# A planned attention-and-MLP kernel: P as a ring of 18 blocks, another rule for VectorE's score steps, another price for an exponential

## The chip, the cores and the metric

One core of one Trainium2 chip. The time is the device time of one execution in microseconds (us), as a median of runs. Engines: TensorE (PE; its weight loads are listed as PEld), VectorE (DVE), ScalarE (ACT), GpSimd (POOL), and SyncE (SP), which issues most DMAs. PSUM has eight banks of 512 fp32 columns, numbered 0 to 7 below.

## What is computed

Cut to what matters (S = 2048, D = 512, 32 heads of 16, one shared K and V head; Fh = 688):

```python
q = (x @ wq) -> 32 heads;  k = x @ wk;  v = x @ wv
p = softmax(einsum('bhqd,bkd->bhqk', q, k) * 16 ** -0.5)
a = einsum('bhqk,bkd->bhqd', p, v) -> (S, 512) @ wo
z = gelu(x @ w_in);  z1, z2 = z[..., :Fh], layernorm(z[..., Fh:])
b = (z1 * (w_sp @ z2 + b_sp[:, None])) @ w_out
g = sigmoid((x * gate_w).sum(-1, keepdims=True))
out = g * a + (1 - g) * b
```

All inputs and the output are bf16.

## The kernel before

**Units and blocks.** The attention is cut into 32 units: a unit u is one chunk of 512 queries and four heads. A *block* is one head's scores of a unit against 128 keys: a matmul of K (32 x 128) and Q (32 x 512) gives a bank of 128 keys x 512 queries (`s_mm`, rows `ps<-QA,KA`). Four heads stand in the four row groups of TensorE, so up to four such matmuls, one for each group g, run side by side. A unit has 16 key tiles x 4 heads = 64 blocks, and the whole kernel 2048.

**Two ways to an exponential.** Most blocks go to ScalarE: one instruction of two or three banks writes exp to the buffer P (`exp_op`, L738, rows `P<-ps`). The step number k sets its banks, `EB[k % 2]`: banks 2 and 3 (and 4, if it is free) or banks 0 and 1. The rest of the key tiles, at most 8 per unit, go to VectorE as a polynomial: `d_A` (L750) evacuates a block from bank 5 or 4 (`DBK`) with a scale and an offset into UW, `d_u` (L757) squares it, and `d_w` (L763) squares it again, on VectorE or, one block of 512 columns at a time, on GpSimd. Where a second matmul's weights and constants complete the polynomial, TensorE adds small matmuls (`UW,VW`, `QA,KTV`, `CT,SVB`). A key tile of VectorE is called a batch; `batches` counts them.

**P·V.** `o_mm` multiplies a block of P or UW by V, in bank 6, one column group per head. Four such matmuls, one of each head, make a round (`pv_round`, `pv_emit`). At a unit's end VectorE transposes bank 6 (`T`, L775), normalises it with GpSimd's help and transposes it back into OT (L806).

**The other half.** z = gelu(x @ w_in) is computed on TensorE between score steps; all gelu instructions of ScalarE run in one stretch, since they need another activation table. After the layernorm come `g_sp` (`wT,z`) and the output matmuls (`wout,z` and `wo,OT`). These groups (`main`, `outs`, `tails`) are called fill: TensorE works at them one piece at a time.

**The order is planned.** No engine chooses anything at run time. While the program is built, a loop steps three clocks (`free`, for pe, act and dve) in nanoseconds, asks `pe_step`, `act_step` or `dve_step` what its engine does next, and records that instruction; each has a due time from constants such as `C_MM = 216.0`. The recorder `Prog.op` then derives semaphore waits from who wrote and read each key. So a constant of the planner changes the order of the instructions and their split between the engines, not the instructions' own speed. The engines run their lists in order.

**The parts that the change touches:**
- P is `[128, NP, 1536]` with NP = 6: step k uses slot k % 6, whether it fills two or three blocks. Reads and writes are tracked per slot (`("P", k % NP)`), `pleft[k]` counts the blocks of a step that P·V has not read yet, and `act_step` does not plan step k before step k - 6 is fully read.
- `act_period(n)`: 426.7 n + 58 ns, the planned distance of two exponentials of n blocks.
- `pe_work`: after ScalarE's next score step (`if bl:`, which also takes along blocks for VectorE while `d_ready` holds) comes a branch for score blocks of VectorE alone (`if d_ready(now, False)`). It is taken in score mode ("S"), where TensorE has just run scores and need not switch, or when no step of ScalarE is open, in the gelu stretch, or when VectorE is short of work.
- `hungry(now)` is VectorE's planned backlog in ns; so far it only decides on bank 4.
- P·V rounds with fewer than four heads are allowed if `press` holds: the slots of P are nearly all in use.
- A filler matmul on zeros (`CT,zer`, tag "warm") is put in where TensorE's planned load over the last 3.4 us is below `W_MIN`.
- `unit_for_act`, `new_batch`: which key tiles VectorE takes. A tile of the next unit is only taken while more than 64 - 12 of its blocks are left.

At the end (`put_out`) the rows of the output are stored by SP, ACT and POOL queues. A flag of the polynomial's validity is read by all engines; a second program, with its own P·V (L1690), runs only if it is set.

Of the kernel before, what the change touches and what calls it, by code (L numbers as in the profile page):

```python
# [6 lines left out]
ACT = mybir.ActivationFunctionType  # L7
# [7 lines left out]
S = 2048  # L15
# [5 lines left out]
NST = 16  # L21
NU = 32
LN_EPS = 1e-5
NP = 6
ND = 5
NQ = 3
NMAX = 8
Q_B = 0.74
Q_A = 0.4770697274170593
Q_AS = 0.5048945666981567  # L30
# [12 lines left out]
RLAST = 12  # L43
XO = (0, 3, 2, 1)
N0 = 3
HEAD = 45000.0
C_TN = 1250.0
GATE = 20000.0
# [4 lines left out]
WBL = 0.5  # L53
BACK = 8
W_WIN = 3400.0
W_MIN = 0.84
W_GEL = 0.95
INFO = None

# [106 lines left out]
def build_kernel(nc, x_d, wq_d, wk_d, wv_d, wo_d, win_d, wsp_d, bsp_d, wout_d, gw_d, out_d):  # L166
    es = ExitStack()
    with es:
        block = es.enter_context(nc.Block())

        def sb(name, shape, dt):
            return es.enter_context(nc.sbuf_tensor(name, shape, dt))
# [9 lines left out]
        def bkey(b):  # L182
            return ("bk", b)
# [14 lines left out]
        NE = sb("NE", [128, 4, 32], B16)  # L198
        SVB = sb("SVB", [128, NMAX + 1, 32], B16)
        CT = sb("CT", [128, 512], B16)  # L200
        P = sb("P", [128, NP, 1536], B16)
        UW = sb("UW", [128, 2, ND, 2048], F16)
        T1 = sb("T1", [128, 2, 512], F32)
        rc = sb("rc", [128, 2, 16], F32)
# [528 lines left out]
            mm(bank(dst_bank), KA[32 * g:32 * g + 32, e, 128 * kt:128 * kt + 128], QA[32 * g:32 * g + 32, (u // 2) % NQ, :], True, True,  # L733
               kr + [("Q", (u // 2) % NQ)], [key], tp=(32 * g, 0), chan="s", tag="S")

        def exp_op(k, n):
            b0, _ = EB[k % 2]
            op("act", lambda a: a.activation(P[:, k % NP, 0:512 * n], ps[:, 512 * b0:512 * (b0 + n)], ACT.Exp),  # L738
               r=[bkey(b0 + i_) for i_ in range(n)], w=[("P", k % NP)], tag="exp")

        started = set()

# [161 lines left out]
        sdone = {}  # L904
        estart = {}
        eend = {-1: 0.0, -2: 0.0}
        pleft = {}
        db = {"cur": None, "todo": []}
        dbs = {b: {"free": 0.0, "blk": None, "ready": None, "k": None} for b in DBK}
        batches = []  # L910
# [19 lines left out]
        def new_batch(now):  # L930
            if db["todo"]:
                return True
            m = len(batches)
            if m >= ND and dleft.get(m - ND, 0) > 0:
                return False
            ua = unit_for_act()
            for u in (ua, ua + 1):
                if u >= NU:
                    continue
                un = units[u]  # L940
                if un["n"] >= NMAX:
                    continue
                rem = rem_of(u)
                if u == ua and rem < (RLAST if u == NU - 1 else RMIN) + 4:
                    continue
                if u > ua and rem <= 64 - 12:
                    continue
                q = when(("Q", u // 2), ("K%d" % (u % 2), 3))
                if q is None or q > now:
                    continue  # L950
                if max(un["nx"]) >= un["hi"]:
                    continue
                kt = NKT - 1 - un["n"]
                if u == 0:
                    ix = O0.index(kt)
                    if kt < NKT - N0 or max(un["nx"]) > ix:
                        continue
                    O0.pop(ix)
                un["hi"] -= 1
                un["n"] += 1  # L960
                batches.append((u, kt, []))
                dleft[m] = 8
                pq[m] = [0, 0, 0, 0.0, 0.0, 0]
                db["cur"] = m
                db["todo"] = [0, 1, 2, 3]
                return True
            return False
# [18 lines left out]
        def hungry(now):  # L986
            return max(0.0, free["dve"] - now) + dve_backlog(now) + 600.0 * sum(d["blk"] is not None for d in dbs.values())
# [54 lines left out]
            return bl  # L1042

        def act_period(n):
            return 426.7 * n + 58.0

        def limit(now):
            k = st_["kf"]
# [42 lines left out]
        def pv_emit(pu, rnd, t_end):  # L1091
            for g, it in rnd:
                pv_items[pu][g].remove(it)
                pv_done[pu] += 1
                pv_g[pu][g] += 1
                it[1](st_["ua"] > pu and pv_g[pu][g] == unit_total(pu) // 4)
                if it[3] is not None:
                    kind, ix = it[3]
                    if kind == "P":
                        pleft[ix] -= 1  # L1100
                        if pleft[ix] == 0:
                            T[("Pfree", ix)] = t_end + 250.0
                    else:
                        dleft[ix] -= 1
            tot = unit_total(pu)
            if pv_done[pu] == tot and pv_const[pu]:
                st_["pu"] += 1
                unit_end(pu, t_end + L_PE)
# [166 lines left out]
        def pe_work(now):  # L1275
# [9 lines left out]
            def sw(m):  # L1285
                return 0.0 if m == mode else C_SW
# [46 lines left out]
                    return t_end  # L1333
            if d_ready(now, False):
                slack = max(0.0, free["dve"] - now) + dve_backlog(now)
                if mode == "S" or topen is None or gst["on"] or (slack < D_SL and now + sw("S") + C_MM <= lim + C_SW):
                    t_end = now + sw("S") + C_MM
                    used = []
                    while d_ready(now, False):
                        used.append(d_emit(used, now, t_end))  # L1340
                    st_["mode"] = "S"
                    return t_end
# [13 lines left out]
            if pv is not None:  # L1356
                rnd, tot, mx = pv
                pu = st_["pu"]
                oldest = min([ix for ix in pleft if pleft[ix] > 0] or [10 ** 9])
                press = st_["ke"] + 1 - oldest >= NP  # L1360
                ending = st_["ua"] > pu and unit_total(pu) - pv_done[pu] <= tot + 8
                urgent = press or ending
            defer = fp is not None and fp[2] is None and not urgent and pv is not None and tot < BACK
# [23 lines left out]
        def act_step(now):  # L1387
            if not st_["gate"]:
                t = when("KTV", "SVB", *[("V", c) for c in range(4)])
                if t is not None and t < now + GATE:  # L1390
                    st_["gate"] = True
                    gate()
                    return now + 130.0
            if aevac_q and aevac_q[0][2] <= now:
                c_, f_, t, d_ = aevac_q.popleft()
                f_()
                if d_:
                    d_(now + c_ + 100.0)
                return now + c_
            if gst["arm"] and (gel or dz["i"] < 24 or dz["cur"] is not None or dz["full"]) and st_["ke"] == st_["kf"] or gst["on"]:  # L1400
                r = None
                extra = 0.0 if gst["on"] else 1300.0
                if dz["full"] and dz["full"][0][3] <= now + extra:
                    r = dz_act(now + extra)
                elif gel:
                    c_, f_, _ = gel.popleft()
                    f_()
                    r = now + c_ + extra
                if r is None:
                    return None  # L1410
                gst["on"] = True
                gst["t"] = r
                if not (gel or dz["i"] < 24 or dz["cur"] is not None or dz["full"]):
                    gst["on"] = False
                    r += 1300.0
                return r
            k = st_["ke"]
            if k in sdone and sdone[k] <= now:
                bl = stepb[k]
                if k >= NP and (pleft.get(k - NP, 0) > 0 or T.get(("Pfree", k - NP), 0.0) > now):  # L1420
                    return None
                n = len(bl)
                exp_op(k, n)
                pleft[k] = n
                st_["ke"] += 1
                estart[k] = now
                eend[k] = now + 426.7 * n + 172.0
                for i_, (u, kt, g) in enumerate(bl):
                    src = P[:, k % NP, 512 * i_:512 * i_ + 512]
                    add_item(u, g, (eend[k] + L_X,  # L1430
                                    lambda last, u=u, g=g, kt=kt, src=src, k=k: o_mm(u, g, V1[:, kt, :], src, [("V", kt // 4), ("P", k % NP)], last), ("V", kt // 4), ("P", k)))
                if st_["ua"] >= NU and st_["kf"] == k + 1:
                    T[("Bend", k % 2)] = eend[k] + L_X
                    T[("Bend", 1 - k % 2)] = eend[k - 1] + L_X
                return now + act_period(n)
            return None
# [218 lines left out]
        for u in range(NU):  # L1655
# [30 lines left out]
            for kt in range(NKT):  # L1686
                for g in range(4):
                    mm2(bank(g), KA[32 * g:32 * g + 32, 0, 128 * kt:128 * kt + 128], QA[32 * g:32 * g + 32, 0, :], True, True, ["Q"], ["sc"], (32 * g, 0))
                for h in range(2):
                    op2("act", lambda a, h=h: a.activation(P[:, h, 0:1024], ps[:, 1024 * h:1024 * h + 1024], ACT.Exp), r=["sc"], w=["P"])  # L1690
                for g in range(4):
                    mm2(ps[32 * g:32 * g + 32, 512 * BO:512 * BO + 512], V1[:, kt, :], P[:, g // 2, 512 * (g % 2):512 * (g % 2) + 512],
                        kt == 0, kt == 15, ["P"], [("bk", BO)], (0, 32 * g))
            t1_op(ps2, u)()
            jj, jp = j % 2, j // 2
# [105 lines left out]
```

## Time and profile before

| | us |
|---|---|
| median of 3 runs | 746.19 (745.87 to 746.45) |
| the profiled execution | 748.75 |
| its span, first to last instruction | 746.7 |

| engine | busy us | share of the span |
|---|---|---|
| PE | 727.3 | 97% |
| DVE | 710.2 | 95% |
| ACT | 727.3 | 97% |
| POOL | 232.9 | 31% |

How to read the rows that follow. A group row names line, engine, operation, written and read tiles and shape, then the count, busy time in us and mean ns of one instruction, then the idle time of the engine ahead of them and who ended it. A timeline row begins with its start and length in us and merges like neighbours; it has the shape of its first instruction. A row of windows has the stretch, its length, the busy time (and count) of PE, PEld, DVE, ACT and POOL, the granted TensorE clock, the DMA share and GB/s. Since neighbours on an engine overlap, mean ns times count is more than busy time. Matmul ends are modelled, so a busy PE is not a full PE.

### The profile page before, as it was taken

What the parts mean: (1) busy time and instruction counts of PE and PEld (TensorE: products, weight loads), DVE (VectorE), ACT (ScalarE), POOL (GpSimd) and SP (SyncE); (2) the same over time, 40 slices, a digit from 0 to 9 for tenths busy, and PEclk for the clock granted to TensorE, in tenths of its full rate; (3) what the DMA queues carried; (4) which work ended last, traced back from release to release, by engine and by line L of the source; (5) the groups of instructions that cost most, each with busy time, mean ns of one, the idle gap of its engine ahead of it and who ended that gap; (6) DMA issues with size and microseconds to landing.
All of it is one profiled execution on the core that took longest, in us unless ns stands there. A gap on an engine that the chain in (4) does not pass through costs nothing.

```text
span 746.7 us, 21174 instructions
## 1 busy us (share of the span) xinstructions
PE 727.3 (97%) x8969; PEld 212.0 (28%) x8969; DVE 710.2 (95%) x980; ACT 727.3 (97%) x749; POOL 232.9 (31%) x241
## 2 busy tenths in 40 slices
PE   8999999999999999999999999999999999999996
PEld 2323233323323222222222222222222222222221
DVE  5799999998999999999999999999999999999996
ACT  5999999999999999999999999999999999999995
POOL 4744324360222322436223343212215131150101
PEclk8999999999999999999999999999999999999999
DMA  8350000000000000500000051000001400000001
GB/s 185 105 113 2 2 3 1 2 2 2 2 2 1 2 2 2 115 21 9 2 1 2 3 92 44 9 3 1 2 2 29 100 8 9 2 3 1 2 2 33
DMA packets 48445, 17.20 MB, mean 23 GB/s; under 512 B 44164, under 2 KB 47800, under 8 KB 48344
## 3 DMA queue, kind: packets, MB, share of 16 engines
q1 hardware_dynamic: 46040, 15.36, 9.0%
q8 instruction: 71, 1.16, 0.7%
q10 hardware_dynamic: 2256, 0.30, 0.3%
q14 instruction: 30, 0.25, 0.1%
q0 software_dynamic: 48, 0.13, 0.0%
HBM read 3.20 MB, written 2.10 MB: 7 GB/s over the span
## 4 chain that ended last, share of the span: by engine, by line
PE 60%; ACT 21%; DVE 11%; issue 8%; POOL 0%; ACTq 0%; POOLq 0%; DVEq 0%
PE ps L348 59%; ACT P L738 20%; DVE UW L750 4%; DVE UW L757 2%; DVE UW L763 1%; DVE bst L592 1%; PE ps L347 1%; DVE T L775 1%; DVE z L578 0%; DVE QA L465 0%; ACT z L586 0%; POOL UW L763 0%; DVE km L447 0%; ACT z L1265 0%; DVE mv L596 0%
## 5 line engine op out<-in xcount | busy, mean ns | idle before, releaser
L738 ACT ACTIVATE P<-ps 128x1024 bf16<-128x1024 f32 (+1 forms) x729 | 701.1, 1242 | 8.0 <-PE ps L348 7.8
L750 DVE TENSOR_SCALAR UW<-ps 128x512 f16<-128x512 f32 (+1 forms) x409 | 329.7, 818 | 14.9 <-PE ps L348 9.9
L348 PE MATMUL ps<-QA,KA 32*128 32x512 bf16 x2048 | 313.0, 386 | 9.5 <-ACT P L738 6.0
L763 POOL TENSOR_TENSOR UW<-UW 128x512 f16<-128x512 f16 x86 | 130.1, 1512 | 308.0 <-DVE UW L750 131.6
L348 PE MATMUL ps<-P,V 128*32 128x512 bf16 x1532 | 224.4, 387 | 0.4 <-DVE T L775 0.2
L348 PEld LDWEIGHTS ps<-QA,KA 32*128 32x128 bf16 x2048 | 84.2, 91 | 307.9 <-ACT P L738 163.1
L757 DVE TENSOR_TENSOR UW<-UW 128x2048 f16<-128x2048 f16 (+1 forms) x147 | 159.9, 1088 | 1.5
L763 DVE TENSOR_TENSOR UW<-UW 128x2048 f16<-128x2048 f16 (+3 forms) x143 | 136.6, 963 | 0.9 <-POOL UW L763 0.8
L348 PE MATMUL ps<-wT,z 128*32 128x512 bf16 x1536 | 131.9, 383 | 0.0
L348 PE MATMUL ps<-UW,VW 128*32 128x512 f16 x516 | 99.9, 385 | 0.0
L348 PE MATMUL ps<-UW,V 128*32 128x512 f16 x516 | 85.3, 387 | 0.5 <-DVE UW L757 0.4
L348 PEld LDWEIGHTS ps<-P,V 128*32 128x32 bf16 x1532 | 54.3, 94 | 60.5 <-issue 53.2
L469 POOL TENSOR_TENSOR QSQ<-QA 128x512 bf16<-128x512 bf16 x16 | 26.1, 1629 | 84.1 <-DVE UW L750 43.4
L348 PEld LDWEIGHTS ps<-wT,z 128*32 128x32 bf16 x1536 | 32.5, 95 | 38.6 <-issue 34.2
L348 PE MATMUL ps<-wout,z 128*32 128x512 bf16 x384 | 33.3, 383 | 0.0
L798 POOL TENSOR_TENSOR Tn<-T,rc 128x512 bf16<-128x512 f32 x15 | 28.2, 1879 | 9.7 <-DVE UW L750 8.9
L348 PEld LDWEIGHTS ps<-UW,VW 128*32 128x32 bf16 x516 | 24.7, 94 | 20.5 <-issue 15.6
L348 PE MATMUL ps<-win,xT 128*32 128x344 bf16 x512 | 30.2, 313 | 0.0
L348 PEld LDWEIGHTS ps<-UW,V 128*32 128x32 bf16 x516 | 20.7, 93 | 24.1 <-issue 17.5
L811 POOL TENSOR_SCALAR gtmp<-T,thr 128x32 f32<-128x32 f32 x16 | 6.7, 418 | 66.3 <-DVE T L775 65.5
L348 PE MATMUL ps<-QA,KTV 128*32 128x512 bf16 x128 | 25.9, 383 | 0.0
L348 PE MATMUL ps<-xT,win 128*32 128x512 bf16 x384 | 24.0, 381 | 0.7 <-ACT z L1265 0.7
(115 smaller groups left out, 401.9 us busy)
## 6 DMA issues: line engine op xcount, KB each, us to landing
out_dram<-outsb SPq DMA_DIRECT2D x14, 128.0 KB, 1.7
win<-in_B_w_in_dram SPq DMA_DIRECT2D x1, 1376.0 KB, 6.0
wout<-in_B_w_out_dram SPq DMA_DIRECT2D x1, 640.0 KB, 5.2
wo<-in_A_wo_dram SPq DMA_DIRECT2D x8, 64.0 KB, 2.3
UW<-in_A_wq_dram SPq DMA_DIRECT2D x1, 384.0 KB, 4.1
wT<-in_B_w_sp_dram SPq DMA_TRANSPOSE x16, 4.4
UW<-in_A_wq_dram ACTq DMA_DIRECT2D x1, 128.0 KB, 4.0
out_dram<-outsb ACTq DMA_DIRECT2D x1, 128.0 KB, 3.7
```

The source lines that it names most:

```text
L347: return t.matmul(dst, lhsT, rhs, start=start, stop=stop)
L348: return t.matmul(dst, lhsT, rhs, start=start, stop=stop, tile_position=tp)
L469: dq(pl_q, 1050.0, lambda: op("pool", lambda v: v.tensor_tensor(QSQ[:, q % 2, :], QA[:, q % NQ, :], QA[:, q % NQ, :], ALU.mult), r=[("Q", ...
L592: dq(dve_q, 410.0, lambda st=st, h=h: op("dve", lambda v: v.bn_stats(bst[:, st, h, :], z2[:, FH * st + 344 * h:FH * st + 344 * h + 344]), ...
L738: op("act", lambda a: a.activation(P[:, k % NP, 0:512 * n], ps[:, 512 * b0:512 * (b0 + n)], ACT.Exp), r=[bkey(b0 + i_) for i_ in range(n)] ...
L750: op("dve", lambda v: v.tensor_scalar(UW[:, 0, s, 512 * i:512 * (i + n)], bank(b, 512 * n), Q_A, Q_AS, ALU.mult, ALU.add), r=[bkey(b + j) ...
L757: op("dve", lambda v: v.tensor_tensor(src, src, src, ALU.mult), r=k, w=k, tag="dTT")
L763: op(eng, lambda v: v.tensor_tensor(UW[:, 1, s, 512 * a:512 * b], src, src, ALU.mult), r=[("U", s, h) for h in range(a // 2, (b + 1) // 2) ...
L775: return lambda: pgx.op("dve", lambda v: v.transpose(T1[:, jj, c0:c1], bank(BO, c1 - c0, c0)), r=[bkey(BO)], w=[("T1", jj, c0)], tag="T1")
L798: pgx.op(eng, lambda v: v.tensor_tensor(tnv[:, pr, j0:j1, b0:b1, :], t1v[:, j0:j1, b0:b1, 0:16], rc[:, j0:j1, b0:b1].unsqueeze(3).broadcas ...
L811: op("pool", lambda v: v.tensor_scalar(gtmp[:], t1v[:, jj, :, 17:19], thr[:, 0:1], None, ALU.is_le), r=[("T1", jj, 0), "thr"], w=["gtmp"], ...
```

## The change

P becomes one line of 18 blocks of 512 columns. An exponential of n blocks takes the next n of them in a row (from the start again where n do not fit), and each block is released by its own P·V matmul. `press` holds when five or fewer blocks are free. The planned distance of two exponentials is 426.7 n + 52 ns (`A_OV`). In score mode VectorE's blocks alone are taken only if `hungry(now)` is under 1000 ns (`D_HG`). `W_MIN` goes from 0.84 to 0.86; the 12 in `new_batch` gets a name and stays 12.

```diff
-NP = 6
+PB = 18
+PRESS = 5
+NXT = 12
+A_OV = 52.0
+D_HG = 1000.0
-W_MIN = 0.84
+W_MIN = 0.86
...
-        P = sb("P", [128, NP, 1536], B16)
+        P = sb("P", [128, 512 * PB], B16)
...
-        def exp_op(k, n):
+        def exp_op(k, n, p0):
             b0, _ = EB[k % 2]
-            op("act", lambda a: a.activation(P[:, k % NP, 0:512 * n], ps[:, 512 * b0:512 * (b0 + n)], ACT.Exp),
-               r=[bkey(b0 + i_) for i_ in range(n)], w=[("P", k % NP)], tag="exp")
+            op("act", lambda a: a.activation(P[:, 512 * p0:512 * (p0 + n)], ps[:, 512 * b0:512 * (b0 + n)], ACT.Exp),
+               r=[bkey(b0 + i_) for i_ in range(n)], w=[("P", p0 + i_) for i_ in range(n)], tag="exp")
...
-        pleft = {}
+        pbusy_ = [False] * PB
+        pfree_ = [0.0] * PB
+        ppos = [0]
+
+        def p_alloc(n, now):
+            p0 = ppos[0] if ppos[0] + n <= PB else 0
+            if any(pbusy_[i] or pfree_[i] > now for i in range(p0, p0 + n)):
+                return None
+            return p0
...
         def act_period(n):
-            return 426.7 * n + 58.0
+            return 426.7 * n + A_OV
...
                     if kind == "P":
-                        pleft[ix] -= 1
-                        if pleft[ix] == 0:
-                            T[("Pfree", ix)] = t_end + 250.0
+                        pbusy_[ix] = False
+                        pfree_[ix] = t_end + 250.0
...
-                if mode == "S" or topen is None or gst["on"] or (slack < D_SL and now + sw("S") + C_MM <= lim + C_SW):
+                if mode == "S" and hungry(now) < D_HG or topen is None or gst["on"] or (slack < D_SL and now + sw("S") + C_MM <= lim + C_SW):
...
-                oldest = min([ix for ix in pleft if pleft[ix] > 0] or [10 ** 9])
-                press = st_["ke"] + 1 - oldest >= NP
+                press = PB - sum(pbusy_) <= PRESS
...
-                if k >= NP and (pleft.get(k - NP, 0) > 0 or T.get(("Pfree", k - NP), 0.0) > now):
+                n = len(bl)
+                p0 = p_alloc(n, now)
+                if p0 is None:
                     return None
-                n = len(bl)
-                exp_op(k, n)
-                pleft[k] = n
+                exp_op(k, n, p0)
+                ppos[0] = p0 + n
+                for i_ in range(n):
+                    pbusy_[p0 + i_] = True
...
-                    src = P[:, k % NP, 512 * i_:512 * i_ + 512]
+                    src = P[:, 512 * (p0 + i_):512 * (p0 + i_) + 512]
                     add_item(u, g, (eend[k] + L_X,
-                                    lambda last, u=u, g=g, kt=kt, src=src, k=k: o_mm(u, g, V1[:, kt, :], src, [("V", kt // 4), ("P", k % NP)], last), ("V", kt // 4), ("P", k)))
+                                    lambda last, u=u, g=g, kt=kt, src=src, ix=p0 + i_: o_mm(u, g, V1[:, kt, :], src, [("V", kt // 4), ("P", ix)], last), ("V", kt // 4), ("P", p0 + i_)))
```

The second program's use of P is rewritten for the new shape in the same way.

More of the change, by code (lines that the diff above doesn't have):

```diff
@@ L945, in new_batch @@
                     continue
-                if u > ua and rem <= 64 - 12:
+                if u > ua and rem <= 64 - NXT:
                     continue
@@ L1689, in build_kernel @@
                 for h in range(2):
-                    op2("act", lambda a, h=h: a.activation(P[:, h, 0:1024], ps[:, 1024 * h:1024 * h + 1024], ACT.Exp), r=["sc"], w=["P"])
+                    op2("act", lambda a, h=h: a.activation(P[:, 1024 * h:1024 * h + 1024], ps[:, 1024 * h:1024 * h + 1024], ACT.Exp), r=["sc"], w=["P"])
                 for g in range(4):
-                    mm2(ps[32 * g:32 * g + 32, 512 * BO:512 * BO + 512], V1[:, kt, :], P[:, g // 2, 512 * (g % 2):512 * (g % 2) + 512],
+                    mm2(ps[32 * g:32 * g + 32, 512 * BO:512 * BO + 512], V1[:, kt, :], P[:, 512 * g:512 * g + 512],
                         kt == 0, kt == 15, ["P"], [("bk", BO)], (0, 32 * g))
```

## The prediction

> **What bounds the kernel now.** The page's busy shares come first. They do not name a bound: three engines stand within two points of each other.
>
> ```profile
> PE 727.3 (97%) x8969; PEld 212.0 (28%) x8969; DVE 710.2 (95%) x980; ACT 727.3 (97%) x749; POOL 232.9 (31%) x241
> ```
>
> So the second view is ScalarE's timeline, merged: one row for each stretch in which it never stood still, with the idle time ahead of it in brackets.
>
> ```profile
> 9.79 5.28 ACT L738 ACTIVATE P<-ps 128x1536 bf16<-128x1536 f32 x5 [5.51 <-PE ps L348]
> 15.53 1.94 ACT L738 ACTIVATE P<-ps 128x1024 bf16<-128x1024 f32 x2 [0.46 <-PE ps L348]
> 17.77 1.02 ACT L738 ACTIVATE P<-ps 128x1024 bf16<-128x1024 f32 x1 [0.31 <-PE ps L348]
> 19.29 1.02 ACT L738 ACTIVATE P<-ps 128x1024 bf16<-128x1024 f32 x1 [0.49 <-PE ps L348]
> 20.80 10.57 ACT L738 ACTIVATE P<-ps 128x1024 bf16<-128x1024 f32 x10 [0.49 <-PE ps L348]
> ...
> 58.75 2.36 ACT L738 ACTIVATE P<-ps 128x1536 bf16<-128x1536 f32 x2 [0.40 <-PE ps L348]
> 61.28 112.78 ACT L738 ACTIVATE P<-ps 128x1024 bf16<-128x1024 f32 x119 [0.16 <-PE ps L348]
> 174.08 1.28 ACT L586 ACT_TABLE_LOAD   x1
> ...
> 195.01 2.14 ACT L1265 ACTIVATE z<-ps 128x1536 bf16<-128x1536 f32 x2 [0.53 <-PE ps L348]
> ...
> 198.46 539.33 ACT L738 ACTIVATE P<-ps 128x1024 bf16<-128x1024 f32 x562
> ```
>
> From 61.28 us to the gelu at 174.08 us, and from 198.46 to 737.79 us, ScalarE goes from one exponential into the next with no gap. A row can hide stalls inside it if instructions stretch, so the third view is the pace: two stretches with 1024-column exponentials alone, and the groups by shape of the last long stretch.
>
> ```profile
> 105.07 41.56 ACT L738 ACTIVATE P<-ps 128x1024 bf16<-128x1024 f32 x45
> ...
> 541.33 41.62 ACT L738 ACTIVATE P<-ps 128x1024 bf16<-128x1024 f32 x45
> ```
>
> ```profile
> L738 ACT ACTIVATE P<-ps 128x1024 bf16<-128x1024 f32 x504 | 478.5, 1206 | 0.0
> L738 ACT ACTIVATE P<-ps 128x1536 bf16<-128x1536 f32 x57 | 92.5, 1622 | 0.0
> L738 ACT ACTIVATE P<-ps 128x512 bf16<-128x512 f32 x1 | 0.8, 812 | 0.0
> ```
>
> A mean duration of 1206 ns is not the pace, because neighbours overlap. The pace is (41.62 - 1.21) / 44 = 0.918 us per 1024-column instruction, and from the 539.33 us stretch (539.33 - 0.8 - 504 x 0.918) / 57 = 1.331 us per 1536-column one. The difference for 512 more columns is 0.413 us, so a 1024-column instruction is some 0.83 us of columns and under 0.1 us of its own: there is no room for a stall in it. Whose turn is late shows in the waits, as total us, times, longest:
>
> ```profile
> PEld ps L348 <- ACT P L738: 164.4, 386, 1.3
> PEld ps L348 <- DVE UW L750: 82.3, 207, 1.1
> ...
> ACT P L738 <- PE ps L348: 7.8, 7, 5.5
> ```
>
> TensorE's weight loads are released by ScalarE 386 times; ScalarE waits seven times, all of them in the rows above, up to 61.28 us. ScalarE's string of exponentials sets the time; TensorE and VectorE fit around it.
>
> **Removed, added, moved.** The planner runs while the program is built, so the costs come from the built order of both kernels (counts, no times). Exponentials of 1024 columns go from 651 to 670, of 1536 from 76 to 66, of 512 stay 2: 9 more instructions and 8 more blocks of 512 columns, 1532 to 1540. These are two key tiles of four blocks that VectorE's polynomial gives up (129 tiles to 127). On ScalarE this is 19 x 0.918 - 10 x 1.331 = 17.4 - 13.3 = **+4.1 us**, all on the path. The stretch at 105.07 us gives 0.917 and 1.340 us by the same steps, and 17.4 - 13.4 = 4.0; these are the bounds.
>
> [...]
>
> The ring itself: block-wise release can only help an exponential that waits for its place in P. Such a wait would be among the seven waits above, and these are at 9.79 to 61.28 us. TensorE's order is the same in both programs up to the matmuls of this row, where 24 become 20, so the first five waits stand ahead of the first change:
>
> ```profile
> 23.67 0.32 PE L348 MATMUL ps<-V,KN 128*32 128x32 bf16 x24
> ```
>
> The wait that the ring adds is for the last reader of the blocks to be overwritten; behind it on ScalarE queue the next exponentials, and TensorE's scores wait for those. But 18 blocks hold nine exponentials of 1024 columns where six slots held six, so it comes later than the old one. I price it 0; the bounds are in the stalls below. The planner's new pace, its backlog rule and its filler threshold act through the order alone, which the following terms count. SP's queue keeps its order and no transfer is added or moved on any queue by name; the gelu's instructions keep their shapes and number.
>
> VectorE: evacuations of 512 columns go from 302 to 238, of 1024 from 107 to 135; squarings have 3 blocks of 512 more, net, as GpSimd does 67 of them instead of 86.
>
> ```profile
> L750 DVE TENSOR_SCALAR UW<-ps 128x512 f16<-128x512 f32 x302 | 200.2, 679 | 13.1 <-PE ps L348 8.6
> L757 DVE TENSOR_TENSOR UW<-UW 128x2048 f16<-128x2048 f16 x111 | 135.3, 1219 | 1.0
> L763 POOL TENSOR_TENSOR UW<-UW 128x512 f16<-128x512 f16 x86 | 130.1, 1512 | 308.0 <-DVE UW L750 131.6 <-DVE UW L757 126.2 <-PE ps L348 34.1
> L750 DVE TENSOR_SCALAR UW<-ps 128x1024 f16<-128x1024 f32 x107 | 129.5, 1210 | 1.8 <-PE ps L348 1.3
> L763 DVE TENSOR_TENSOR UW<-UW 128x1024 f16<-128x1024 f16 x40 | 27.1, 678 | 0.0
> L348 PE MATMUL ps<-CT,zer 128*32 128x512 bf16 x116 | 9.8, 382 | 0.0
> ```
>
> By busy time per instruction that is 28 x 1.21 - 64 x 0.663 = -8.5 us, and 3 x 0.30 = +0.9 us for the squarings: VectorE is relieved of 7.6 us. GpSimd loses 19 x 1.51 = 28.7 us. TensorE loses 28 matmuls, of them 20 fillers at 9.8 / 116, or 1.7 us. All three lie under ScalarE's string, so I count **0**; without that cover VectorE's part would be worth the 7.6 us.
>
> Stalls of ScalarE. The idle time of the rows from 15.53 to 61.28 us sums to 2.31 us, of it 1.75 in the unchanged part and 0.56 at 58.75 and 61.28 us; ahead of the last gelu it is 0.53. Around 40 to 80 us VectorE is full and stays the late engine there:
>
> ```profile
> 10.00:20.00 10.00, 8.99 (x131) 2.04 (x123) 5.98 (x13) 8.69 (x9) 5.35 (x11) 0.70 0.89 217
> 40.00:80.00 40.00, 38.81 (x460) 12.24 (x452) 39.90 (x59) 39.36 (x42) 19.11 (x21) 1.00 0.19 41
> ```
>
> (us, then busy time of PE, PEld, DVE, ACT, POOL, then clock.) From 40 to 80 us VectorE is busy 39.90 of 40. The new order there has the same kinds of work, so I leave these stalls where they are: **0**, with -1.1 (both groups gone) and +2.2 (twice as much again) as bounds.
>
> **The tail.** The end of the run, before:
>
> ```profile
> 725.17 12.61 ACT L738 ACTIVATE P<-ps 128x1024 bf16<-128x1024 f32 x13
> ...
> 733.57 0.68 DVE L750 TENSOR_SCALAR UW<-ps 128x512 f16<-128x512 f32 x1
> 734.28 1.22 DVE L757 TENSOR_TENSOR UW<-UW 128x2048 f16<-128x2048 f16 x1
> 735.54 1.23 DVE L763 TENSOR_TENSOR UW<-UW 128x2048 f16<-128x2048 f16 x1
> 738.28 0.78 DVE L775 STREAM_TRANSPOSE T<-ps 128x256 f32<-128x256 f32 x2 [1.51 <-PE ps L348]
> ```
>
> The last exponential ends at 737.78, VectorE's last squaring already at 736.77; after the last P·V matmul the transposes start at 738.28. In the new order VectorE's last score block again stands with the fourth exponential from the end, but behind its evacuation come one squaring of 1024 columns and three of 2048, where there were two of 2048: 0.68 + 1.22 = 1.90 us more. VectorE would end near 738.67 on the old clock. With some 0.5 us for the last matmuls behind it (738.28 - 737.78 is that step for ScalarE), the transposes start near 739.2: **+0.9 us**. Bounds: 0 if VectorE has caught up by then, 1.9 if nothing of it is hidden.
>
> **Sum.** 4.1 + 0 + 0 + 0.9 = +5.0 us. The profiled execution took 748.75 us (span 746.7 and 2.05 around it), so its like would take 753.75; the median of the runs shown, 746.19, lies 2.56 below the profiled one. The forecast is 746.19 + 5.0 = **751.2 us**.
>
> **The rivals.**
> Closed gaps (not slower): the new order feeds ScalarE without its early waits and the tail stays as it was. Place: 15.53 to 61.28 us and 195.01 us; price 2.31 + 0.53 = 2.84 us back, against +4.1: 746.19 + 1.3 = 747.5 us. It decides from about 2.6 us returned. Against it: 1.75 of the 2.84 us lie ahead of the first changed instruction. For it: VectorE has less to do.
>
> VectorE is the real bound (faster): its 95% would then be worth the 7.6 us, 746.19 - 7.6 = 738.6 us. ScalarE's gapless 539.33 us speak against it, and with them it could not come true while ScalarE gets 8 more blocks.
>
> Scores held up by VectorE's banks (slower still): runs of four score matmuls go from 111 to 167, in which VectorE's blocks stand ahead of ScalarE's on TensorE's in-order queue; a bank not yet evacuated (207 such releases now) then delays both. Price: the small gap 0.16 us at 56 runs is 9.0 us, 751.2 + 9.0 = 760.2 us. Against it: VectorE has more slack than before, and since 61.28 us no such delay reached ScalarE.
>
> Clock drops: with 20 filler matmuls fewer, TensorE's granted clock falls once in the middle. The row from 10 to 20 us shows 0.70, six of the ten us at half speed, and ScalarE's four gaps there are 1.75 us: 751.2 + 1.75 = 753.0 us for each fall. [...]
>
> Not what it says: the ring and the exponential's new price change only the order; if the planner had kept its shares, +4.1 would be absent and 746.2 us remain. The counts of the built order exclude it.
>
> **How the numbers follow.** Forecast 77%, its own range 749.1 to 753.3 (the bounds summed, with half of the stalls' upper one: 4.0 - 1.1 + 0 to 4.1 + 1.1 + 1.9). Scores held up 8%, clock 6%, closed gaps 6%, VectorE the bound 3%. The measurement tells 0.2%, 1.5 us, from no change. Closed gaps is inside this (747.5 < 747.7), so same 0.06; faster 0.03; the rest, 0.91, slower. The range takes in the bounds, one clock fall and the smaller half of held-up scores: 748.4 to 755.
>
> **What would show it.** Right: no idle time of ScalarE between about 65 us and the end beside the gelu; 0.918 us per 1024-column exponential; the string of exponentials some 4 us longer; transposes about 1.4 us behind the last exponential instead of 0.5. Wrong: ScalarE's waits for TensorE above ten in number (held-up scores), a clock below 1.00 in a window after 40 us, or an early stretch without the gaps at 15 to 61 us. The forecast falls if the 738 exponentials fit into the old span, because then the pace of 0.918 us was not ScalarE's own.

## The result and the profile after

| | kernel before | changed kernel |
|---|---|---|
| median of 5 runs, us | 746.19 (745.87 to 746.45) | 750.05 (749.55 to 751.98) |
| the profiled execution, us | 748.75 | 750.48 |
| its span, us | 746.7 | 748.7 |

The ratio is 1.0056, with a 95% interval of 1.0044 to 1.0067: 3.9 us slower, inside the range and 1.15 us below the forecast. The two profiled executions differ by 1.7 us only, because the one of before ran its head at half clock (0.50 from 13.96 to 20.78 us) and the changed one did not (1.00 there; last section).

Busy shares of the changed kernel, from the page:

```profile
PE 728.7 (97%) x8941; PEld 208.7 (28%) x8941; DVE 706.7 (94%) x945; ACT 730.9 (98%) x758; POOL 194.4 (26%) x222
```

VectorE lost 3.5 us of busy time and GpSimd 38.5, ScalarE gained 3.6. ScalarE's timeline, merged as in the prediction (start, length, first shape, count, idle time ahead in brackets):

```profile
9.35 5.28 ACT L742 ACTIVATE P<-ps 128x1536 bf16<-128x1536 f32 x5 [5.07 <-PE ps L352]
15.44 12.93 ACT L742 ACTIVATE P<-ps 128x1024 bf16<-128x1024 f32 x13 [0.81 <-PE ps L352]
28.62 154.84 ACT L742 ACTIVATE P<-ps 128x1536 bf16<-128x1536 f32 x162
...
207.47 531.68 ACT L742 ACTIVATE P<-ps 128x1024 bf16<-128x1024 f32 x558
```

From 28.62 us on there is no idle time named in front of an exponential, and the last one ends at 207.47 + 531.68 = 739.15 us (737.79 before). The pace is taken from the groups by shape of the last stretch, and the waits of ScalarE (total us, times, longest) follow:

```profile
L742 ACT ACTIVATE P<-ps 128x1024 bf16<-128x1024 f32 x509 | 482.7, 1283 | 0.0
L742 ACT ACTIVATE P<-ps 128x1536 bf16<-128x1536 f32 x48 | 81.1, 1689 | 0.0
...
L742 ACT ACTIVATE P<-ps 128x512 bf16<-128x512 f32 x1 | 0.9, 858 | 0.0
```

```profile
ACT P L742 <- PE ps L352: 5.9, 2, 5.1
```

By the prediction's steps, (531.68 - 0.9 - 509 x 0.918) / 48 = 1.324 us per 1536-column exponential, where it was 1.331. Both carry the 0.918 over from the prediction; read directly from the ends of neighbours behind 210 us, the median distances are 917 and 1344 ns (917 and 1343 before). So the mean duration rose from 1206 to 1283 ns, but the distance between neighbours is the same. ScalarE waits twice, not seven times. VectorE at the end, from its timeline:

```profile
735.67 0.68 DVE L767 TENSOR_TENSOR UW<-UW 128x1024 f16<-128x1024 f16 x1
736.27 1.22 DVE L761 TENSOR_TENSOR UW<-UW 128x2048 f16<-128x2048 f16 x1
737.40 2.35 DVE L767 TENSOR_TENSOR UW<-UW 128x2048 f16<-128x2048 f16 x2
740.47 0.78 DVE L779 STREAM_TRANSPOSE T<-ps 128x256 f32<-128x256 f32 x2 [0.71 <-PE ps L352]
```

The last squaring ends at 739.75 us, 0.6 us behind the last exponential (1.0 us ahead of it before). The transposes start 1.32 us behind the last exponential (0.49 before).

### The profile page after: what moved, and what is told of

Its sections match the earlier page's. It is cut to its first block, busy times and chain, and to the rows that moved or that the text cites. A ratio compares the mean times of both kernels' runs of the same rounds, so it can differ in the third digit from the quotient of the medians.

```text
span 748.7 us, 21003 instructions
## 1 busy us (share of the span) xinstructions
PE 728.7 (97%) x8941; PEld 208.7 (28%) x8941; DVE 706.7 (94%) x945; ACT 730.9 (98%) x758; POOL 194.4 (26%) x222
## 4 chain that ended last, share of the span: by engine, by line
PE 70%; ACT 14%; DVE 8%; issue 6%; POOL 1%; DMA 1%; ACTq 0%; POOLq 0%; DVEq 0%
PE ps L352 70%; ACT P L742 14%; DVE UW L754 3%; DVE bst L596 2%; DVE UW L761 1%; DMA xT<-in_A_x_dram 1%; POOL z L529 1%; DVE UW L767 1%; ACT z L590 0%; DVE mv L600 0%; POOL UW L767 0%; DVE km L451 0%; DVE QA L469 0%; ACT L590 0%; POOL QSQ L473 0%
## 5 line engine op out<-in xcount | busy, mean ns | idle before, releaser
L754 DVE TENSOR_SCALAR UW<-ps 128x512 f16<-128x512 f32 (+1 forms) x373 | 322.5, 874 | 23.6 <-PE ps L352 19.0
L352 PE MATMUL ps<-P,V 128*32 128x512 bf16 x1540 | 218.1, 386 | 1.0 <-issue 0.7
L352 PEld LDWEIGHTS ps<-QA,KA 32*128 32x128 bf16 x2048 | 86.5, 91 | 324.8 <-ACT P L742 181.0
L767 POOL TENSOR_TENSOR UW<-UW 128x512 f16<-128x512 f16 x67 | 90.3, 1347 | 317.1 <-DVE UW L761 155.5
L761 DVE TENSOR_TENSOR UW<-UW 128x2048 f16<-128x2048 f16 (+1 forms) x146 | 158.2, 1084 | 1.1
L767 DVE TENSOR_TENSOR UW<-UW 128x2048 f16<-128x2048 f16 (+3 forms) x145 | 140.6, 973 | 0.1
L352 PE MATMUL ps<-UW,VW 128*32 128x512 f16 x508 | 96.6, 385 | 0.2 <-POOL z L529 0.2
L352 PEld LDWEIGHTS ps<-P,V 128*32 128x32 bf16 x1540 | 50.9, 94 | 61.9 <-issue 57.6
L815 POOL TENSOR_SCALAR gtmp<-T,thr 128x32 f32<-128x32 f32 x16 | 9.2, 572 | 98.5 <-DVE T L779 92.1
```

What stands on the lines that cost most here:

```text
L352: return t.matmul(dst, lhsT, rhs, start=start, stop=stop, tile_position=tp)
L754: op("dve", lambda v: v.tensor_scalar(UW[:, 0, s, 512 * i:512 * (i + n)], bank(b, 512 * n), Q_A, Q_AS, ALU.mult, ALU.add), r=[bkey(b + j) ...
L761: op("dve", lambda v: v.tensor_tensor(src, src, src, ALU.mult), r=k, w=k, tag="dTT")
L767: op(eng, lambda v: v.tensor_tensor(UW[:, 1, s, 512 * a:512 * b], src, src, ALU.mult), r=[("U", s, h) for h in range(a // 2, (b + 1) // 2) ...
L815: op("pool", lambda v: v.tensor_scalar(gtmp[:], t1v[:, jj, :, 17:19], thr[:, 0:1], None, ALU.is_le), r=[("T1", jj, 0), "thr"], w=["gtmp"], ...
```

## The experiments

One account serves all of them. *String*: the exponentials of the built order times the distance between the ends of neighbours (0.917, 1.343 and 0.489 us for 1024, 1536 and 512 columns). *Stalls*: what the exponentials took beyond that. *Tail*: from the end of the last exponential to the end of the span. *Fill left*: matmuls of the MLP, the output and the flag that stand behind the last score matmul in TensorE's built order. The kernels without the two engines' added work, by fill left:

| kernel | string | stalls before and after the gelu | last exponential ends | fill left | tail | median |
|---|---|---|---|---|---|---|
| last_unit | 705.7 | 0.95, -0.13 | 740.34 | 16 | 8.29 | 750.48 |
| four_consts | 704.1 | 0.67, 0.03 | 739.96 | 28 | 8.67 | 749.90 |
| pace_46 | 707.5 | 1.80, -0.15 | 743.99 | 32 | 8.40 | 754.51 |
| before | 700.0 | 3.36, 0.01 | 737.79 | 36 | 8.86 | 746.19 |
| changed | 704.0 | 1.71, -0.13 | 739.15 | 36 | 9.54 | 750.05 |
| retuned | 698.3 | 0.28, 0.30 | 732.41 | 36 | 9.65 | 743.65 |
| rule_only | 703.7 | 0.57, -0.16 | 737.97 | 44 | 8.45 | 748.21 |
| pace_64 | 698.2 | 0.91, 1.29 | 735.03 | 141 | 16.69 | 752.69 |
| ring_only | 700.0 | 1.19, 1.08 | 737.09 | 145 | 15.62 | 754.56 |
| two_consts | 699.9 | 1.76, 0.10 | 736.00 | 165 | 18.71 | 756.53 |
| hg_off | 700.3 | 0.91, -0.16 | 734.73 | 201 | 21.16 | 758.18 |

The first theory was that of the prediction: the string alone, so whatever gives ScalarE fewer blocks is faster.

**The changed kernel without the backlog rule (hg_off)**

```diff
-D_HG = 1000.0
+D_HG = 1e9
```

> The change with the backlog rule undone (D_HG so high that it never holds): by the built order 668 exponentials of 1024 columns, 65 of 1536, 1 of 512, so 1532 blocks on ScalarE as before. Theory (ScalarE's string sets the time, 0.918 us and 1.331 us each): 17 more of 1024 and 11 fewer of 1536 than before are 15.6 - 14.6 = +1.0 us, with one of 512 fewer +0.5, so about 746.7 us, and 3.4 us under the changed kernel. Rival (the time comes from the order, from scores held up or the tail, not from the count of blocks): within 1 us of the changed kernel's 750.05 us. Rival (VectorE is the bound): VectorE has 394 evacuations against 373 and more time to spend, so slower than 750.05 us.

**The ring alone (ring_only)**, with the old planned pace and filler threshold:

```diff
-A_OV = 52.0
-D_HG = 1000.0
+A_OV = 58.0
+D_HG = 1e9
-W_MIN = 0.86
+W_MIN = 0.84
```

> The ring alone, with the old price of an exponential (58 ns), the old filler threshold and no backlog rule: 650 exponentials of 1024, 77 of 1536, 1 of 512. Theory: 1 fewer of 1024, 1 more of 1536, 1 fewer of 512 are -0.9 + 1.3 - 0.5 = -0.1 us, so 746.1 us; the ring by itself is worth nothing because ScalarE never waited for its place in P. Rival (the ring brings or costs something by itself): more than 1.5 us away from 746.2 us.

**The ring with a longer planned exponential (pace_64)**, without the rule and with a lower filler threshold

```diff
-A_OV = 52.0
-D_HG = 1000.0
+A_OV = 63.7
+D_HG = 1e9
-W_MIN = 0.86
+W_MIN = 0.80
```

> The ring with the planner's price of an exponential at 426.7 n + 63.7 ns, which is the measured 0.917 us for two blocks, no backlog rule, filler threshold 0.80: 652 exponentials of 1024, 74 of 1536, 2 of 512, so 1528 blocks, one key tile fewer on ScalarE than before. Theory: 1 more of 1024 and 2 fewer of 1536 are +0.9 - 2.7 = -1.8 us, so 744.4 us. Rival (VectorE is the bound, it has 409 evacuations and one key tile more): slower than before, 747 us or more.

Measured: hg_off 758.18 us (757.96 to 760.45), ratio 1.0165 [1.0147, 1.0183]; ring_only 754.56 us (754.50 to 756.83), 1.0121 [1.0103, 1.0139]; pace_64 752.69 us (752.31 to 753.54), 1.0084 [1.0069, 1.0098]. All three miss by 8 to 11.5 us. By their times alone, hg_off and pace_64 would also fit the rival that VectorE is the bound. But the string did what was expected: in hg_off the last exponential ends 4.4 us earlier than in the changed kernel. The time is lost behind it. TensorE, VectorE and ScalarE in the tail of hg_off, from the timeline:

```profile
736.61 0.69 DVE L754 TENSOR_SCALAR UW<-ps 128x512 f16<-128x512 f32 x1 [0.21 <-PE ps L352]
...
739.25 0.45 DVE L779 STREAM_TRANSPOSE T<-ps 128x256 f32<-128x256 f32 x1 [0.49 <-PE ps L352]
739.62 0.64 DVE L632 TENSOR_TENSOR z<-ps,z 48x512 bf16<-48x512 f32 x1
...
740.32 1.48 PE L352 MATMUL ps<-wout,z 128*32 128x512 bf16 x24 [0.90 <-DVE z L632]
...
742.50 0.75 DVE L656 TENSOR_SCALAR z<-ps,G 128x512 f32<-128x512 f32 x1 [0.69 <-PE ps L352]
...
743.31 1.48 PE L352 MATMUL ps<-wout,z 128*32 128x512 bf16 x24 [0.86 <-DVE z L656]
...
745.49 0.75 DVE L656 TENSOR_SCALAR z<-ps,G 128x512 f32<-128x512 f32 x1 [1.88 <-PE ps L352]
...
746.69 1.48 PE L352 MATMUL ps<-wout,z 128*32 128x512 bf16 x24 [0.24 <-DVE flag L726]
748.00 1.04 PE L352 MATMUL ps<-wo,OT 128*32 128x512 bf16 x16
748.86 1.47 PE L352 MATMUL ps<-wout,z 128*32 128x512 bf16 x24
749.09 0.69 ACT L700 ACTIVATE outsb<-ps,G 128x512 bf16<-128x512 f32 x1 [14.36 <-PE ps L352]
```

The MLP's output groups are still to be done: 24 matmuls, an evacuation by VectorE, 24 matmuls, an evacuation, each waiting for the one before. ScalarE stands still for 14.36 us. The work of TensorE from 210 to 725 us shows where it fell behind. Rows of windows (length, busy time and count of PE, PEld, DVE, ACT and POOL, clock), first of the changed kernel, then of hg_off:

```profile
210.00:725.00 515.00, 511.12 (x5998) 138.16 (x5998) 494.22 (x615) 515.00 (x541) 116.73 (x104) 1.00 0.08 17
```

```profile
210.00:725.00 515.00, 508.86 (x5842) 139.10 (x5842) 499.18 (x623) 515.00 (x542) 153.39 (x127) 1.00 0.08 17
```

TensorE is as busy and its clock is the same, but it finishes 156 matmuls fewer, and hg_off has 165 more left at the end. Counted from the start of each piece of work to the start of the next, the scores took 197.7 us in hg_off (1512 matmuls) and 187.7 us in the changed kernel (1506): runs of three are 236 instead of 178 and took 390 ns each instead of 360. What is neither score, P·V, polynomial nor filler had 168.8 us instead of 178.3. ScalarE is busy all the time in both. So the first theory falls, and the second is: time = string + few stalls + a tail that is 8 to 10 us while the fill is nearly done, and grows by (21.16 - 8.45) / (201 - 44) = 0.08 us for each further fill matmul. Not all of this is fill: in the four late kernels the transposes start 2.4 to 4.5 us behind the last exponential (0.5 to 1.3 in the others), and in hg_off VectorE evacuates its last score block 1.9 us behind ScalarE's end. Behind the start of the transposes the four still need 12.8 to 16.6 us, the others 7.8 to 8.6.

**A shorter planned exponential and a tighter rule (pace_46)**, which give ScalarE still more blocks:

```diff
-A_OV = 52.0
-D_HG = 1000.0
+A_OV = 46.0
+D_HG = 600.0
-W_MIN = 0.86
+W_MIN = 0.82
```

> The change pushed further the same way: price 426.7 n + 46 ns, backlog rule at 600 ns, threshold 0.82: 667 exponentials of 1024, 71 of 1536, 1 of 512, so 1548 blocks, two key tiles more than the changed kernel. Theory: 16 more of 1024, 5 fewer of 1536, 1 fewer of 512 than before are 14.7 - 6.7 - 0.5 = +7.5 us, so 753.7 us. Rival (the changed kernel's loss is its order or its tail): near 750 us. Rival (VectorE is the bound): VectorE has four key tiles fewer than before, so faster than 746 us.

Measured 754.51 us (754.18 to 756.90), ratio 1.0121 [1.0101, 1.0140], as expected. The string is 3.5 us longer than in the changed kernel, the fill is done (32 left), and the tail is 8.40. The rival that VectorE is the bound falls here: VectorE has four key tiles fewer than before, and the kernel is 8.4 us slower.

**The kernel before with the rule alone (rule_only)**: six slots of P, 58 ns and 0.84 as before.

```diff
-                if mode == "S" or topen is None or gst["on"] or (slack < D_SL and now + sw("S") + C_MM <= lim + C_SW):
+                if mode == "S" and hungry(now) < 1000.0 or topen is None or gst["on"] or (slack < D_SL and now + sw("S") + C_MM <= lim + C_SW):
```

> The kernel before with the backlog rule alone (D_HG = 1000 in its own planner; slots of P, 58 ns and W_MIN 0.84 as before). In its built order ScalarE has 657 exponentials of 1024 columns, 75 of 1536 and one of 512 (string 703.7 us by 0.917, 1.343 and 0.489 us, against 700.0 of before), and 44 fill matmuls stand behind the last score matmul (36 before). Theory (time = ScalarE's string + its few stalls + a tail that grows with the fill left behind the last scores): the rule alone costs nearly all of the change, +3.7 us of string and about +0.5 us of tail, 749.5 to 751 us. Rival (the ring with its finer release is what costs, and the rule gives back): without the ring 745 to 747 us.

Measured 748.21 us (747.98 to 748.53), ratio 1.0030 [1.0019, 1.0041]: above the rival, but 1.3 us below the theory's lower end. String and fill came as built; the stalls, the gelu's stretch (23.96 us, 24.39 before) and the tail came shorter than the theory allowed. So the rule costs 2.3 us by itself, and the ring with the two constants adds some 1.6 us to it in the changed kernel; these 1.6 us were not taken apart further.

**Two groups of constants, and both (two_consts, four_consts, retuned)**. `D_SL` lets VectorE's blocks through outside score mode when VectorE's planned slack is below it (-1: never). `HALF` is the time within which a score block must come for VectorE not to go on squaring instead. P·V waits behind a piece of fill while fewer than `BACK` of its matmuls are ready. In the last unit VectorE takes no new key tile when fewer than `RLAST` + 4 blocks are left. The first group:

```diff
-A_OV = 52.0
-D_HG = 1000.0
+A_OV = 62.0
+D_HG = 2500.0
```

> The changed kernel with A_OV = 62 and D_HG = 2500 alone. String 699.9 us by its counts (647, 79 and one), but 165 fill matmuls are left behind the last score matmul. Theory: the string ends about 4 us earlier than in the changed kernel, the tail is between the 16.7 us of 141 left (the ring with A_OV = 63.7) and the 21.2 us of 201 left (the ring and 52 ns without the rule), about 18.5: 754 to 756 us, slower than the changed kernel. Rival (left-over fill is not what sets the tail): 746 to 747 us, the changed kernel less the 4.1 us of string.

The second group:

```diff
-D_SL = -1.0
-HALF = 500.0
-RLAST = 12
-BACK = 8
+D_SL = 200.0
+HALF = 300.0
+RLAST = 8
+BACK = 12
```

> The changed kernel with D_SL = 200, HALF = 300, BACK = 12 and RLAST = 8 alone. String 704.1 us by its counts (676, 62 and two), 28 fill matmuls left. Theory: nothing gained in the string, the early stalls of ScalarE (1.71 us in the changed kernel) at most closed, tail 8.3 to 9.7 us: 748 to 750 us; the 743.65 us of all six constants together needs both groups, the first for the string and the second so that the fill is done in time. Rival (the gain of the six is in the fewer stalls, not in the string): 744 to 746 us.

All six:

> The changed kernel with six planner constants set otherwise (price 426.7 n + 62 ns, backlog rule at 2500 ns, and four others), chosen by two counts of the built order: ScalarE's string, 655 exponentials of 1024, 72 of 1536, 2 of 512, so 1528 blocks, and the fill matmuls behind the last score matmul, 36 as in the kernel before and in the changed one (201, 145 and 141 in the three runs that ended 8 to 12 us late). Two-term theory (time = ScalarE's string plus the tail behind it, and the tail is long where fill is left over): 4 more of 1024 and 4 fewer of 1536 than before are 3.7 - 5.3 = -1.7 us, tail as before, so 744.4 us. Rival (VectorE's extra key tile makes it late): 748 us or more. Rival (fill left over does not matter): the same 744.4 us, so this run does not test it by itself; the three late runs do.

Measured: two_consts 756.53 us (756.33 to 758.64), ratio 1.0151 [1.0134, 1.0168], tail 18.71; four_consts 749.90 us (749.56 to 750.41), 1.0051 [1.0035, 1.0068]; retuned **743.65 us** (743.55 to 744.26), 0.9969 [0.9957, 0.9981]. The first group saves the string and pays for it in the tail, 0.5 us over the theory's upper end; the second gets the fill done and saves nothing of the string. Together they are faster than both kernels, although VectorE has one key tile more than before, so that rival falls too: ScalarE has 1528 blocks in the built order (1532 before), and its timeline shows a single wait of 0.24 us after the start.

```profile
28.73 138.00 ACT L742 ACTIVATE P<-ps 128x1024 bf16<-128x1024 f32 x142
...
190.70 190.74 ACT L742 ACTIVATE P<-ps 128x1024 bf16<-128x1024 f32 x200
381.68 350.73 ACT L742 ACTIVATE P<-ps 128x1024 bf16<-128x1024 f32 x368 [0.24 <-PE ps L352]
```

**Work added to ScalarE (add_act)**, in `exp_op` of the kernel before; the output stays as it is:

```diff
+            if k >= 64 and k % 8 == 7:
+                op("act", lambda a: a.activation(wk_sb[:].rearrange("p a d -> p (a d)"), zer[:, 0:64], ACT.Exp), r=["zer"], w=["wk"], tag="xa")
```

> The kernel before with 83 dummy exponentials of 64 columns on ScalarE (one behind each eighth exponential from the 64th on), nothing else changed; the planner does not know of them. At 0.12 us each (64 columns at 0.83 ns and the 0.064 us of its own that the pace of 0.917 us leaves) that is 10 us. Theory (ScalarE's string sets the time): all of it shows, 754 to 758 us. Rival (VectorE or TensorE is the bound): under 2 us, 748 us at most.

Measured 756.86 us (756.70 to 759.38), ratio 1.0156 [1.0136, 1.0176]: 10.9 us for 83 instructions, 0.13 us each. None of it is absorbed. ScalarE has no slack. The added group shows again that a duration is no price (457 ns each):

```profile
L741 ACT ACTIVATE wk_sb<-zer 128x64 bf16<-128x64 bf16 x83 | 37.9, 457 | 0.0
```

**Work added to VectorE (add_dve)**, in `d_A` of the kernel before; again the output stays:

```diff
+            if m == 20 and i + n == 4:
+                op("dve", lambda v: v.memset(wk_rep[:], 0.0), w=[("wk_rep", 0)], tag="xd")
+            if m > 20 and m % 3 == 2 and i + n == 4:
+                x = wk_rep[:].rearrange("p a n -> p (a n)").bitcast(F16)
+                op("dve", lambda v: v.tensor_tensor(x, x, x, ALU.mult), r=[("wk_rep", 0)], w=[("wk_rep", 0)], tag="xd")
```

> The kernel before with 36 dummy multiplications of 512 columns (f16) on VectorE, one behind the last evacuation of each third key tile from the 21st on, and one memset; the planner does not know of them. At 0.33 us each that is 12 us. Theory (VectorE lies under ScalarE's string and has idle time): at most 3 us show, 746 to 749 us. Rival (VectorE is a bound of its own): 8 us or more, 754 us or more.

The added group, and ScalarE's timeline behind the gelu:

```profile
L756 DVE TENSOR_TENSOR wk_rep<-wk_rep 128x512 f16<-128x512 f16 x36 | 15.2, 423 | 0.0
```

```profile
196.63 223.90 ACT L738 ACTIVATE P<-ps 128x1024 bf16<-128x1024 f32 x231
420.92 30.97 ACT L738 ACTIVATE P<-ps 128x1024 bf16<-128x1024 f32 x32 [0.39 <-PE ps L348]
452.12 206.93 ACT L738 ACTIVATE P<-ps 128x1536 bf16<-128x1536 f32 x215 [0.23 <-PE ps L348]
659.27 80.52 ACT L738 ACTIVATE P<-ps 128x1024 bf16<-128x1024 f32 x84 [0.22 <-PE ps L348]
```

Measured 749.99 us (749.71 to 750.12), ratio 1.0051 [1.0036, 1.0067]: 4.06 us for 15.2 us of work, between theory and rival. VectorE has cover for about 11 us of it; at the expectation's 0.33 us each (the 12 squarings of 512 columns in before's trace end a median of 0.33 us behind their neighbours) the work is 12 us and the cover, as an estimate, 8. The rest appears as 3.84 us of ScalarE's stalls behind the gelu: 0.84 us are the three gaps in the rows, the other 3.0 lie inside stretches that look gapless, as longer distances between exponentials.

**No late tile for VectorE in the last unit (last_unit)**, a change to the changed kernel's tail:

```diff
-RLAST = 12
+RLAST = 20
```

> The changed kernel with RLAST 20 for 12: in the last unit one key tile moves from VectorE to ScalarE. 668 exponentials of 1024, 69 of 1536, 1 of 512: 2 fewer of 1024, 3 more of 1536, 1 fewer of 512 than the changed kernel are -1.8 + 4.0 - 0.5 = +1.7 us of string. Theory of the tail (the transposes come late in the changed kernel because VectorE still squares behind the last exponential): the step from the last exponential to the transposes falls from 1.3 to about 0.5 us, so 750.05 + 1.7 - 0.8 = 750.9 us. Rival (the tail is the same whatever VectorE has left): 751.8 us and a step of 1.3 us.

VectorE at the end, from its timeline:

```profile
733.80 1.23 DVE L767 TENSOR_TENSOR UW<-UW 128x2048 f16<-128x2048 f16 x1
740.83 0.78 DVE L779 STREAM_TRANSPOSE T<-ps 128x256 f32<-128x256 f32 x2 [5.80 <-PE ps L352]
```

Measured 750.48 us (750.34 to 751.47), ratio 1.0063 [1.0047, 1.0079]. VectorE is done 5.3 us ahead of the last exponential (740.34), and the step to the transposes is 0.49 us again. It gains nothing, because ScalarE gets the tile instead: string 705.7.

## Why the prediction was right, and where it was not

- *The bound.* Right, and now shown by intervention: all of add_act's work came out in the time. No run adds work to TensorE alone, so its slack was not measured.
- *ScalarE's string, +4.1 us.* Right: 704.0 - 700.0 = +4.0 us, at an unchanged pace. The prediction's 1.331 us for 1536 columns, a remainder, is 1.343 when read directly, which takes off the 0.1. From the two distances, as an estimate, a column takes 0.83 ns ((1343 - 917) / 512, the figure of add_act's expectation), and 65 ns of the 917 stand beside the columns (917 - 2 x 426): the prediction's "under 0.1 us of its own" holds.
- *The tail, +0.9 us.* Right, mechanism and size: the transposes come 1.32 instead of 0.49 us behind the last exponential, +0.83, and last_unit takes this back by taking VectorE's late work away. The tail as a whole grew by 9.54 - 8.86 = 0.68 us.
- *VectorE's relief, 0.* Right: before, no stall of ScalarE on its exponentials after 61.28 us was there to be removed. The size is not right: VectorE's busy time fell by 3.5 us, not 7.6. The converse would have been wrong: add_dve shows that VectorE has only some 8 to 11 us of cover.
- *The ring, 0; TensorE "under ScalarE's string".* The sum came out right here, but with luck, since the step is incomplete. The prediction looked for what the ring could do to ScalarE's waits and for TensorE's busy time, never for whether TensorE's fill is finished when the scores are. It is, in before and changed alike (36 matmuls left). Ring alone, with as many blocks for ScalarE as before, is 8.5 us slower than before, 6.8 us of it in the tail (15.62 against 8.86), and the rule that costs ScalarE 8 blocks is what gets the fill done. The parts do not add: ring +8.5, rule +2.3, everything but the rule +12.1, all together +3.9 us. Why TensorE gets fewer matmuls done in the same busy time with the ring and without the rule stays open. In hg_off the score runs take longer than in the changed kernel; between ring_only and before the scores differ by 2.6 us only (193.9 against 191.3, from 210 to 725 us), and each fill matmul takes 77 ns instead of 73. The runs of four do not explain it: the four kernels with much fill left have 127 to 131 runs of four score matmuls in the built order, retuned, rule_only, four_consts, pace_46 and the changed kernel 149 to 172, but before has only 111 and its fill is done.
- *The stalls, 0.* As a sum nearly right, for another reason than given. Profile against profile they fell from 3.36 to 1.71 us. Of the fall of 1.65, 1.75 us was the group "in the unchanged part", which the prediction took for a property of the order; it belongs to the half clock of that one execution (add_act, which is the kernel before up to 82 us, has the clock at 1.00 from 10 to 20 us and runs 19 exponentials from 9.64 us without a gap; so does add_dve, also at 1.00, from 9.75 us, whose TensorE and ScalarE have the order of before throughout).
- *The size, 5.0 against 3.9.* From profile to profile the span grew by 4.0 of string - 1.65 of stalls before the gelu - 0.14 after it - 0.38 of the gelu's stretch - 0.44 of a first exponential that starts earlier + 0.68 of tail = 2.07 us (748.7 - 746.65 = 2.05). With the 1.75 us of the head given back, that is 3.8; but the head cost more than these gaps, some 2.4 us (last section), so this agreement is in part luck. Between ordinary executions the span grew by 4.4 us (743.9, the median of the 30 in the last section, to 748.3), and the time around it fell by 0.3 (2.1 to 1.75), which the prediction took to stay the same. The rest of what the prediction lacked are small terms: string and tail 0.1 and 0.2 shorter than priced, the gelu's stretch and the start. Over the eleven later kernels' traces the first exponential starts anywhere from 9.29 to 9.93 us and the gelu's stretch takes 23.95 to 25.36, so neither was worked out as an effect of the change. Terms of this size also move from one execution to the next: last_unit, which has the changed kernel's order on TensorE and ScalarE up to the last unit, starts 0.25 us later and has 0.95 us of early stalls instead of 1.71.
- *The rivals.* Closed gaps: the gaps did go from the trace, but only the profiled execution had most of them. VectorE the bound, scores held up (9.0 us priced; ScalarE waits twice) and "not what it says" fell. No clock drop came in the changed kernel from 40 us to 746 us, with 20 fillers fewer; behind that its clock is 0.50, as before's is behind 744.4 us. But the rival is real: pace_64 has such a drop from 610.71 to 614.12 us. ScalarE's two gaps in it are 0.39 and 0.49 us, about 0.9 us, where 1.75 was priced from a half clock that lasted twice as long. What brings a fall on is not shown: this one and the one in before's head came behind stretches in which TensorE was busy for 2.57 of 3.41 and 2.44 of 3.42 us (rows in the last section).

## What to carry to other kernels

When several engines are at 95% and more, a change is not priced until each of them has been asked for what it will still have to do when the bounding engine is finished: count that work in the built order, because busy time does not show it. A part of a change can be worth nothing or 8 us according to the parts it comes with, so try each part alone and in place before calling it free. Before using a profiled execution's gaps, see whether its clock row is that of an ordinary run.

## What the runs showed of the hardware

**A half-clock head in some executions.** The profile of before has the clock at 0.70 from 10 to 20 us; the changed kernel's row for this stretch is

```profile
10.00:20.00 10.00, 8.32 (x198) 3.06 (x194) 6.96 (x15) 9.13 (x11) 5.23 (x12) 1.00 0.91 196
```

TensorE does 198 matmuls there, where it did 131, at a similar busy time. In before's trace the half clock lasts from 13.96 to 20.78 us. These are the rows of that stretch and of the one ahead of it, then the same for the drop in pace_64:

```profile
10.54:13.96 3.42, 2.44 (x81) 1.11 (x84) 1.46 (x6) 3.36 (x4) 3.06 (x7) 1.00 1.08 169
13.96:20.78 6.82, 6.82 (x65) 1.17 (x69) 4.42 (x7) 5.09 (x6) 1.83 (x4) 0.50 0.70 227
```

```profile
607.30:610.71 3.41, 2.57 (x30) 0.68 (x30) 3.41 (x6) 3.41 (x5) 1.87 (x4) 1.00 0.08 26
610.71:614.12 3.41, 3.41 (x32) 0.59 (x30) 2.40 (x4) 2.53 (x4) 1.97 (x1) 0.50 0.06 17
```

Ahead of the two falls TensorE's longest gap is 0.79 and 0.53 us. In pace_46 it is busy for only 1.96 of 3.41 us from 185.50 us on, with one gap of 1.45 us, and the clock stays at 1.00; in these three stretches busy time alone therefore does not decide it.

Among 33 later executions of the kernel before, three had a mean clock of 0.994 and took 748.20 to 748.50 us, as the profiled one did; the other 30, at 0.997 to 0.999, took 745.2 to 746.4. The changed kernel's run of 751.98 us has 0.994 too. Where the clock fell in these four no trace shows; by their mean clock they are like the profiled one. So the head costs, as an estimate from these times, some 2.4 us when it comes, which accounts for nearly all of the 2.56 us by which the profiled execution of before lay above the median. What brings it on was not found.

**The length of an instruction and the distance of two.** In the changed kernel the mean duration of a 1024-column exponential rose by 77 ns and the distance between the ends of neighbours did not change (0.917 us). Only the distance can be added up.
